# Talking-heads attention and a leaky MLP: cast and remainder of a regrouped tile two groups ahead of its mixing, and a weight piece narrowed every third step

## The chip, the cores and the metric

One core of one Trainium2 chip runs the whole program. The time is device microseconds from the first to the last instruction of one execution, as the median of several runs. The engines are TensorE (PE for its matmuls, PEld for its weight loads), VectorE (DVE), ScalarE (ACT), GpSimd (POOL) and SyncE (SP), which issues nearly all DMAs from one queue.

## The reference

```python
def _attn_ref(q, k, v, w_pre, w_post):              # q, k, v: 4 x 12 x 448 x 64
    scores = scale * np.matmul(q, k.transpose(0, 1, 3, 2))
    scores = np.einsum('bhij,hg->bgij', scores, w_pre)
    scores = scores - np.max(scores, axis=-1, keepdims=True)
    attn = np.exp(scores)
    attn = attn / (np.sum(attn, axis=-1, keepdims=True) + 1e-09)
    attn = np.einsum('bhij,hg->bgij', attn, w_post)
    return np.matmul(attn, v)

def _moe_ref(x, w_in, w_out):                       # x: 1792 x 768, w_in: 768 x 2048
    h = x @ w_in
    return np.maximum(0.01 * h, h) @ w_out
```

The output of the attention, with the heads side by side, is the `x` of the MLP. The MLP's weights arrive as 64-bit floats, two 32-bit words each, and the kernel has to make 32-bit floats of them: it calls that narrowing.

## The kernel before

**Attention.** The 448 queries of each of the 4 batches are cut into chunks of 120, 120, 120 and 88 rows, 16 chunks in all. A chunk is walked in 12 slots (`t` in the main loop). In slots 0 to 5 `scores(n + 1, h)` makes the scores of two heads of the next chunk: two matmuls into `pss` (the query as a rounded part `qhi` and a remainder `qlo`), copied by ScalarE into `st`. At the end of slot 5 all twelve heads are there, and `regroup` (line 205) starts transfers from `st` to tiles `rt` in which 10 queries by 12 heads lie on 120 partitions: four at slot 5, two each at slots 7, 8, 9 and 10. `softmax(n, s, g)` takes one such group: ScalarE rounds `rt` to `rhi` (line 218), the remainder `rlo` is made by GpSimd, or by VectorE where g is 3 (line 219), three matmuls mix the heads into `psm` in the order hi, lo, hi (line 222), VectorE takes the maximum (223), ScalarE the exponential (224), and after the last group of four the normalising factors go into `kp` (235 to 237). In slot t the loop calls `softmax` for a group that is four slots ahead: in slots 6 and 7 the last two of chunk n, in slots 8 to 11 the first four of chunk n + 1. `mix` (264, copied out at 272) mixes the heads again three slots behind the slot, and `values` (290) multiplies by v in slots 6 to 11. I call slots 6 to 9, where the work goes over from one chunk's groups to the next one's, the turn.

In slot 6 `prep_q(n + 2)` splits the queries of the chunk after next: two casts on ScalarE (`qhi`, line 177) and two subtractions on GpSimd (`qlo`, line 178), half of the heads each. In two of four chunks of a batch `prep_k` splits the keys of the next batch (lines 153 and 154, VectorE and GpSimd).

**Narrowing.** `w_moe` is cut into 64 pieces of 128 x 384 weights: 16 blocks f, of which pieces 0 and 1 are the half for the first matmul and 2 and 3 that for the second. `Narrow` loads one (line 91, 384 KB, tile `craw`), `scale` has two activations on ScalarE (101, 102, into `z` and `w`), `place` three VectorE operations (108, 111, 114, into `top` and `exp`), `join` two GpSimd operations and the store of 192 KB to `w_dram` (117, 118, 119). The first instruction of each stage is pinned by `keep_in_program_order`. Within the attention a piece is started every fifth slot, its stages come four, five and six slots later, and `craw` and `w` have two buffers each: 36 pieces (four each of blocks 0 and 1, two each of the others). The other 28, two each of blocks 2 to 15, are narrowed in the first pass of the MLP, by `load_w` (line 333 and those before it).

**MLP.** 4 batches x 16 blocks: `hidden(i)` is 18 matmuls into `psh`, `project(i)` 18 into `pso` (line 347), each weight split into `wh` and `wl` by VectorE (340, 341). `load_w` reads 384 KB halves `wr` back from `w_dram`, except where the piece is narrowed on the spot.

**What sets the order.** TensorE's instructions run in the order in which the program gives them. On the other engines the framework orders them at build time with its own estimate of the times: of the instructions that it takes to be ready, the one that stands first in the program goes first. On the chip each engine and SyncE's queue then run strictly in that order. The tiles' pools bring the waits: a tile can be written only when the last reader of its buffer is done.

Of the kernel before, what the change touches and what calls it, by code (L numbers as in the profile page):

```python
# [8 lines left out]
F32 = mybir.dt.float32  # L9
F32R = mybir.dt.float32r  # L10
U32 = mybir.dt.uint32
# [12 lines left out]
PIECE = 384  # L24
LATE = 3
EARLY = 2
# [7 lines left out]
def kernel(  # L34
# [10 lines left out]
    nc = tc.nc  # L45
    B, P, NJ, H, D = v.shape
    S = k.shape[3]
# [4 lines left out]
    RH = ROWS * H  # L52
    SLOTS = 3 * NJ
# [25 lines left out]
    class Narrow:  # L79
# [7 lines left out]
        def __init__(self, pool, f, j, w=None):  # L87
            at = slice(PIECE * j, PIECE * (j + 1))
            self.pool, self.w, self.dst = pool, w, w_dram[f][:, at]
            self.raw = pool.tile([P, PIECE, 2], U32, tag="raw", name="craw", bufs=2)  # L90
            nc.sync.dma_start(self.raw.rearrange("p n w -> p (n w)"), w_moe[f, :, at].bitcast(U32))
# [5 lines left out]
        def scale(self, pin):  # L97
            if self.w is None:
                self.w = self.pool.tile([P, PIECE], F32, tag="w", name="w", bufs=2)
# [26 lines left out]
    p_rs = pool("rs", 3)  # L126
# [79 lines left out]

    def softmax(n, s, g):
# [7 lines left out]
        raw = r_t.pop((n, s, g))  # L215
        hi = p_rs.tile([RH, S], F32R, tag="hi", name="rhi")
        lo = p_rs.tile([RH, S], F32R, tag="lo", name="rlo")
        nc.scalar.copy(hi[:kk], raw[:kk])  # L218
        (nc.vector if g == 3 else nc.gpsimd).tensor_sub(lo[:kk], raw[:kk], hi[:kk].bitcast(F32))  # L219
# [205 lines left out]
    for n in range(NCK):  # L425
# [4 lines left out]
        for t in range(SLOTS):  # L430
# [7 lines left out]
            if (n * SLOTS + t) % 5 == 0 and pieces and not last:  # L438
                with tc.issue_after(last_dma[0].ins):
                    narrowing.append(Narrow(p_c, *pieces.pop(0)))  # L440
            if n % NB == NB - 2 and b + 1 < B:
                load_k(b + 1, t)
# [26 lines left out]
            flush = n * SLOTS + t == (NCK - 1) * SLOTS - 1  # L469
            phase = (n * SLOTS + t) % 5  # L470
            if phase == 4 and narrowing:
                narrowing[0].scale(tc.keep_in_program_order)
            if phase == 0 and narrowing and narrowing[0].w is not None or flush and narrowing:
                narrowing[0].place(tc.keep_in_program_order)
            if phase == 1 and narrowing and narrowing[0].w is not None or flush and narrowing:
                narrowing.pop(0).join(tc.keep_in_program_order)
# [95 lines left out]
```

## Time and profile before

| | us |
|---|---|
| median of 3 runs (1104.58 to 1112.42) | 1104.62 |
| the profiled execution, its own time | 1114.43 |
| span of the profiled execution | 1112.7 |
| TensorE busy in the span | 997.6 |
| VectorE busy | 739.7 |
| ScalarE busy | 511.4 |
| GpSimd busy | 431.9 |

The profiled execution took 1114.43 us, 1.7 us more than its span from the first to the last instruction, and 0.9% more than the median. The attention fills the span to about 605 us, the MLP the rest. A matmul's end is modelled in the profile, so a busy TensorE is not TensorE at its peak.

### The profile page before, as it was taken

How to read it: one execution, taken by the hardware profiler on the slowest of the kernel's cores; microseconds unless marked ns; L12 is line 12 of the kernel's file. 1: busy time of each engine (PE TensorE's matmuls, PEld its weight loads, DVE VectorE, ACT ScalarE, POOL GpSimd, SP SyncE). 2: the span in 40 equal slices, each digit the busy share in tenths (PEclk: the TensorE clock that was granted, in tenths of full speed). 3: DMA queues.
4: the chain of work that ended last, by engine and by line, in shares of the span. 5: the costliest groups of instructions: out<-in, count | busy, mean ns of one | idle time of the engine just before them, and what ended most of it. 6: DMA issues, size and time to landing. Idle time of an engine off the chain costs nothing.

```text
span 1112.7 us, 17708 instructions
## 1 busy us (share of the span) xinstructions
PE 997.6 (90%) x6564; PEld 836.3 (75%) x6564; DVE 739.7 (66%) x1210; ACT 511.4 (46%) x1131; POOL 431.9 (39%) x356
## 2 busy tenths in 40 slices
PE   4879689898788997898998988889999999999998
PEld 2667577676566875777777877778999999999997
DVE  5567967569566776666676698797555655565553
ACT  3777577666457775777673333331111211121111
POOL 4576855558556477545542256650000000000000
PEclk9989899988889998999998999999999999999999
DMA  4645534743543564326544566556333633353331
GB/s 159 249 155 190 169 116 157 226 174 101 163 170 113 155 207 161 128 100 207 174 160 140 152 179 192 176 169 208 104 109 104 200 100 113 103 160 100 114 88 62
DMA packets 93770, 167.10 MB, mean 150 GB/s; under 512 B 26740, under 2 KB 68724, under 8 KB 93172
## 3 DMA queue, kind: packets, MB, share of 16 engines
q1 hardware_dynamic: 91956, 163.23, 45.8%
q10 hardware_dynamic: 1728, 2.75, 0.7%
q8 instruction: 51, 0.84, 0.3%
q14 instruction: 35, 0.29, 0.1%
HBM read 103.82 MB, written 23.59 MB: 115 GB/s over the span
## 4 chain that ended last, share of the span: by engine, by line
PE 52%; DVE 15%; DMA 9%; ACT 6%; POOL 5%; issue 5%; SPq 1%; ACTq 0%; POOLq 0%; DVEq 0%
PE psh L347 17%; PE pso L347 16%; PE psa L264 6%; PE psx L290 5%; PE psm L222 5%; DMA craw<-in_w_moe 4%; PE pss L194 3%; DMA w_dram<-w 2%; POOL rlo L219 2%; DMA rt<-st 2%; DVE kst L153 2%; DVE stat L223 2%; DVE wh L340 2%; ACT et L224 2%; POOL qlo L178 1%
## 5 line engine op out<-in xcount | busy, mean ns | idle before, releaser
L219 POOL TENSOR_TENSOR rlo<-rt,rhi 120x448 fp32r<-120x448 f32 x144 | 172.3, 1207 | 117.9 <-ACT rhi L218 109.5
L264 PE MATMUL psa<-kp,et 120*128 120x120 f32 (+2 forms) x1800 | 193.4, 269 | 2.8 <-DVE at L272 2.4
L264 PEld LDWEIGHTS psa<-kp,et 120*128 120x128 f32 (+2 forms) x1800 | 174.5, 179 | 28.5 <-issue 14.0
L340 DVE CAST wh<-wr 128x768 fp32r<-128x768 f32 x128 | 81.9, 640 | 142.0 <-PE psh L347 94.4
L222 PE MATMUL psm<-rhi,kpre 120*120 120x448 f32 x360 | 150.7, 419 | 28.2 <-ACT et L224 14.2
L223 DVE TENSOR_REDUCE stat<-psm 120x1 f32<-120x448 f32 x180 | 111.2, 618 | 70.9 <-PE psm L222 69.8
L347 PE MATMUL pso<-gh,wl 128*128 128x448 f32 x384 | 141.3, 370 | 13.7 <-DVE wl L341 13.7
L358 ACT ACTIVATE t<-psh 128x448 f32<-128x448 f32 x64 | 34.8, 544 | 247.8 <-PE psh L347 247.8
L347 PE MATMUL psh<-xh,wl 128*128 128x448 f32 x384 | 141.7, 369 | 1.9 <-DVE wl L341 1.5
L347 PE MATMUL psh<-xl,wh 128*128 128x448 f32 x384 | 141.2, 368 | 0.0
L347 PE MATMUL pso<-gh,wh 128*128 128x448 f32 x384 | 141.1, 367 | 0.0
L347 PE MATMUL psh<-xh,wh 128*128 128x448 f32 x384 | 141.1, 367 | 0.0
L347 PE MATMUL pso<-gl,wh 128*128 128x448 f32 x384 | 141.1, 367 | 0.0
L224 ACT ACTIVATE et<-psm,stat 120x448 f32<-120x448 f32 x180 | 115.6, 642 | 49.3 <-DVE stat L223 45.2
L218 ACT CAST rhi<-rt 120x448 fp32r<-120x448 f32 x180 | 101.6, 571 | 54.0 <-PE psm L222 27.4
L341 DVE TENSOR_TENSOR wl<-wr,wh 128x768 fp32r<-128x768 f32 x128 | 124.9, 976 | 1.6
L195 ACT ACTIVATE st<-pss 120x448 f32<-120x448 f32 (+1 forms) x192 | 105.8, 557 | 9.0 <-PE pss L194 8.9
L222 PE MATMUL psm<-rlo,kpre 120*120 120x448 f32 x180 | 73.3, 407 | 37.9 <-POOL rlo L219 37.9
L194 PE MATMUL pss<-kst,qlo 128*120 128x448 f32 (+1 forms) x192 | 83.6, 436 | 26.0 <-ACT st L195 14.5
L222 PEld LDWEIGHTS psm<-rhi,kpre 120*120 120x120 f32 x360 | 71.4, 198 | 42.9 <-ACT et L224 18.2
L347 PEld LDWEIGHTS pso<-gh,wl 128*128 128x128 f32 x384 | 72.1, 188 | 25.0 <-issue 18.2
L272 DVE COPY at<-psa 128x480 f32<-128x480 f32 (+2 forms) x112 | 68.2, 609 | 32.3 <-PE psa L264 31.9
(64 smaller groups left out, 1650.5 us busy)
## 6 DMA issues: line engine op xcount, KB each, us to landing
wr<-w_dram SPq DMA_DIRECT2D x114, 384.0 KB
rt<-st SPq DMA_DIRECT2D x176, 210.0 KB
craw<-in_w_moe SPq DMA_DIRECT2D x64, 384.0 KB
kraw<-in_k SPq DMA_DIRECT2D x48, 224.0 KB
qraw<-in_q SPq DMA_DIRECT2D x11, 720.0 KB
w_dram<-w SPq DMA_DIRECT2D x36, 192.0 KB
vt<-in_v SPq DMA_DIRECT2D x4, 1536.0 KB
xr<-x_dram SPq DMA_DIRECT2D x24, 224.0 KB
```

Source lines behind the costliest of these rows:

```text
L194: nc.tensor.matmul(ps[:m, :S], w[:, h, :m], k_t[b, h], start=i == 0, stop=i == 1)
L195: nc.scalar.activation(s_t[n][:m, h, :], ps[:m, :S], AF.Copy, scale=scale)
L218: nc.scalar.copy(hi[:kk], raw[:kk])
L219: (nc.vector if g == 3 else nc.gpsimd).tensor_sub(lo[:kk], raw[:kk], hi[:kk].bitcast(F32))
L222: nc.tensor.matmul(ps[:kk, :S], kpre[w][:kk, :sg[g][1], :], x[:kk], start=i == 0, stop=i == 2)
L223: nc.vector.tensor_reduce(st[:kk, 0, g:g + 1], ps[:kk, :S], axis=AX.X, op=ALU.max, negate=True)
L224: nc.scalar.activation(e[:kk], ps[:kk, :S], AF.Exp, bias=st[:kk, 0, g:g + 1], accum_out=st[:kk, 1, g:g + 1])
L264: nc.tensor.matmul(ps[p0:p0 + np, w * g:w * g + nh * r], es[g][:r * H, c * P:c * P + np], kp[:r * H, g, h::step, :r], start=True, stop=True,)
L272: copy(at[:, :, i:i + full * ROWS].rearrange("p h (g r) -> p g h r", r=ROWS), ps[:, :w * full].rearrange("p (g h r) -> p g h r", h=nh, r=R ...
L340: nc.vector.tensor_copy(hi, raw)
L341: nc.vector.tensor_sub(lo, raw, hi.bitcast(F32))
L347: nc.tensor.matmul(ps, w[a][:, c * P:(c + 1) * P], x[e], start=first and j == 0, stop=last and j == 2)
```

## The change

Two things. The two steps that make `rhi` and `rlo` leave `softmax` for a function `split`, and `softmax` of a group first calls `split` for every group up to two places on in the sequence of all groups, as far as its regrouping was started; the tiles have four buffers in place of three. And a piece of the weights is started every third slot in place of every fifth, with three buffers each for `craw` and `w`; blocks 0 to 13 give four pieces and 14 and 15 two, so 60 of the 64 are narrowed in the attention and four (of blocks 14 and 15) in the MLP. Each piece goes through its stages four, five and six slots after its start, as before, and whatever is left at slot 11 of the last chunk but one is finished there.

```diff
+AHEAD = 2
-EARLY = 2
+EARLY = 14
...
-            self.raw = pool.tile([P, PIECE, 2], U32, tag="raw", name="craw", bufs=2)
+            self.raw = pool.tile([P, PIECE, 2], U32, tag="raw", name="craw", bufs=3)
...
-                self.w = self.pool.tile([P, PIECE], F32, tag="w", name="w", bufs=2)
+                self.w = self.pool.tile([P, PIECE], F32, tag="w", name="w", bufs=3)
...
-    p_rs = pool("rs", 3)
+    p_rs = pool("rs", 4)
...
+    sequence = [(n, s, g) for n in range(NCK) for s in range(3) for g in range(len(chunks[n][3][s]))]
+    split_t = {"next": 0}
+
+    def split(n, s, g):
+        kk = chunks[n][3][s][g][1] * H
+        raw = r_t.pop((n, s, g))
+        hi = p_rs.tile([RH, S], F32R, tag="hi", name="rhi")
+        lo = p_rs.tile([RH, S], F32R, tag="lo", name="rlo")
+        nc.scalar.copy(hi[:kk], raw[:kk])
+        (nc.vector if g == 3 else nc.gpsimd).tensor_sub(lo[:kk], raw[:kk], hi[:kk].bitcast(F32))
+        split_t[n, s, g] = hi, lo
...
-        raw = r_t.pop((n, s, g))
-        hi = p_rs.tile([RH, S], F32R, tag="hi", name="rhi")
-        lo = p_rs.tile([RH, S], F32R, tag="lo", name="rlo")
-        nc.scalar.copy(hi[:kk], raw[:kk])
-        (nc.vector if g == 3 else nc.gpsimd).tensor_sub(lo[:kk], raw[:kk], hi[:kk].bitcast(F32))
+        while split_t["next"] <= min(sequence.index((n, s, g)) + AHEAD, len(sequence) - 1):
+            if sequence[split_t["next"]] not in r_t:
+                break
+            split(*sequence[split_t["next"]])
+            split_t["next"] += 1
+        hi, lo = split_t.pop((n, s, g))
...
-            if (n * SLOTS + t) % 5 == 0 and pieces and not last:
+            if (n * SLOTS + t) % 3 == 0 and pieces and not last:
...
+                    narrowing[-1].at = n * SLOTS + t
...
-            phase = (n * SLOTS + t) % 5
-            if phase == 4 and narrowing:
-                narrowing[0].scale(tc.keep_in_program_order)
-            if phase == 0 and narrowing and narrowing[0].w is not None or flush and narrowing:
-                narrowing[0].place(tc.keep_in_program_order)
-            if phase == 1 and narrowing and narrowing[0].w is not None or flush and narrowing:
-                narrowing.pop(0).join(tc.keep_in_program_order)
+            at = n * SLOTS + t
+            for piece in list(narrowing):
+                while piece.stage < 3 and (piece.stage or at - piece.at >= 4 or at == (NCK - 1) * SLOTS - 1):
+                    (piece.scale, piece.place, piece.join)[piece.stage](tc.keep_in_program_order)
+                    piece.stage += 1
+                    if at < (NCK - 1) * SLOTS - 1:
+                        break
+                if piece.stage == 3:
+                    narrowing.remove(piece)
```

## Rows read from the trace of the kernel before

**Rows 1.** The page: busy time, share of the span and instructions of each engine, and the 40 slices of the span (27.8 us each) for TensorE, and the clock that it was granted (9 is 90% or more of full speed).

```profile
PE 997.6 (90%) x6564; PEld 836.3 (75%) x6564; DVE 739.7 (66%) x1210; ACT 511.4 (46%) x1131; POOL 431.9 (39%) x356
...
PE   4879689898788997898998988889999999999998
...
PEclk9989899988889998999998999999999999999999
```

**Rows 2.** Windows over three stretches, first the attention, then the first steps of the MLP, then the rest of it: start and end, length, then for each engine its busy time and instructions, then the granted clock, the busy share of the DMA engines and GB/s.

```profile
60.00:605.00 545.00, 473.93 (x3991) 374.63 (x3993) 380.20 (x661) 364.21 (x842) 326.40 (x271) 0.92 0.48 158
605.00:750.00 145.00, 129.98 (x718) 114.11 (x714) 117.46 (x188) 47.07 (x99) 73.41 (x56) 1.00 0.55 169
750.00:1108.00 358.00, 357.43 (x1728) 324.18 (x1728) 206.81 (x308) 63.80 (x117) 0.00 (x0) 1.00 0.39 119
```

**Rows 3.** Waits of TensorE's matmuls from 60 to 605 us: who waited for whom, us in total, times, the longest.

```profile
PE psm L222 <- POOL rlo L219: 36.9, 16, 4.6
PE psm L222 <- ACT et L224: 13.8, 9, 2.9
...
PE psm L222 <- ACT rhi L218: 7.2, 5, 2.1
```

**Rows 4.** Windows over four chunks of the attention, each from the first regrouping transfer of one chunk to that of the next (columns as in rows 2).

```profile
87.60:125.28 37.68, 33.01 (x302) 25.50 (x299) 30.14 (x50) 24.87 (x59) 28.11 (x24) 1.00 0.52 173
125.28:161.86 36.58, 29.33 (x234) 23.25 (x234) 25.31 (x42) 23.54 (x54) 23.86 (x20) 0.91 0.49 163
387.03:423.01 35.98, 31.95 (x288) 24.77 (x288) 28.90 (x48) 25.43 (x60) 27.05 (x23) 1.00 0.57 186
495.95:530.88 34.93, 31.34 (x278) 25.44 (x278) 24.66 (x43) 26.78 (x61) 19.50 (x16) 0.95 0.57 189
```

**Rows 5.** Timeline of one turn from chunk to chunk, 494 to 508 us: start and length in us, engine, line, operation, tiles, shapes, count, and in brackets the idle time before it and what ended it.

```profile
495.95 3.28 SPq L205 DMA_DIRECT2D rt<-st  x4
496.27 2.90 ACT L177 CAST qhi<-qraw 128x720 fp32r<-128x720 f32 x2
...
497.84 4.57 POOL L178 TENSOR_TENSOR qlo<-qraw,qhi 128x720 fp32r<-128x720 f32 x2 [5.67 <-ACT qhi L177]
...
499.07 0.64 ACT L224 ACTIVATE et<-psm,stat 120x448 f32<-120x448 f32 x1
...
499.69 0.57 ACT L218 CAST rhi<-rt 120x448 fp32r<-120x448 f32 x1
...
500.31 0.47 PE L222 MATMUL psm<-rhi,kpre 120*120 120x448 f32 x1
...
500.77 1.04 ACT L218 CAST rhi<-rt 120x448 fp32r<-120x448 f32 x2
502.38 1.24 POOL L219 TENSOR_TENSOR rlo<-rt,rhi 120x448 fp32r<-120x448 f32 x1
...
503.67 0.46 PE L222 MATMUL psm<-rlo,kpre 120*120 120x448 f32 x1 [2.89 <-POOL rlo L219]
...
504.55 3.02 POOL L219 TENSOR_TENSOR rlo<-rt,rhi 120x448 fp32r<-120x448 f32 x2
...
507.19 0.71 PE L222 MATMUL psm<-rhi,kpre 120*120 120x448 f32 x1
```

**Rows 6.** Groups of instructions from 60 to 605 us, of every engine: line, engine, operation, tiles, shapes, count, then busy us and mean ns of one, then the idle time of the engine before them and what ended most of it.

```profile
L219 POOL TENSOR_TENSOR rlo<-rt,rhi 120x448 fp32r<-120x448 f32 x135 | 162.1, 1211 | 112.4 <-ACT rhi L218 104.1 <-DMA w_dram<-w 3.3 <-DMA x_dram<-xo 3.0
...
L218 ACT CAST rhi<-rt 120x448 fp32r<-120x448 f32 x165 | 93.1, 571 | 48.0 <-PE psm L222 25.3 <-POOL rlo L219 13.0 <-DMA rt<-st 4.9
...
L178 POOL TENSOR_TENSOR qlo<-qraw,qhi 128x720 fp32r<-128x720 f32 (+1 forms) x26 | 51.3, 1995 | 32.4 <-ACT qhi L177 32.1
...
L118 POOL TENSOR_TENSOR w<-w,top 128x384 f32<-128x384 f32 x36 | 38.5, 1070 | 1.2
L117 POOL TENSOR_TENSOR w<-w,exp 128x384 f32<-128x384 f32 x36 | 37.1, 1031 | 44.0 <-DVE exp L114 36.8 <-PE psm L222 6.1 <-DVE stat L236 0.9
...
L111 DVE SCALAR_TENSOR_TENSOR top<-z,top 128x384 uint32<-128x384 uint32 x35 | 32.1, 917 | 0.4
...
L114 DVE TENSOR_SCALAR exp<-top 128x384 uint32<-128x384 uint32 x35 | 21.3, 609 | 0.4
L101 ACT ACTIVATE z<-craw 128x384 f32<-128x384 f32 x35 | 19.5, 558 | 0.0
L102 ACT ACTIVATE w<-craw 128x384 f32<-128x384 uint32 x34 | 19.0, 560 | 59.1 <-DMA w_dram<-w 32.6 <-DMA craw<-in_w_moe 20.2 <-POOL rlo L219 6.3
...
L108 DVE TENSOR_SCALAR top<-z 128x384 uint32<-128x384 uint32 x35 | 18.0, 514 | 3.8 <-ACT z L101 3.7
```

**Rows 7.** The line of the second step of `place`, over the whole span: shortest, median and longest of one in ns, first and last start, shapes.

```profile
L111 DVE SCALAR_TENSOR_TENSOR top<-z,top x64: 543/550/2316, 54.1 to 744.3; 128x384 uint32<-128x384 uint32 x64
```

**Rows 8.** Waits of SyncE's queue from 60 to 605 us, the longest in total: us, times, the longest.

```profile
SPq L119 <- POOL w L118: 130.1, 25, 12.3
```

**Rows 9.** The chain of waits over the whole span, some pieces of it in the MLP: start, us, what it is.

```profile
666.43 3.14 DMA craw<-in_w_moe
...
675.10 3.13 DMA craw<-in_w_moe
...
773.35 3.72 PE pso L347 x18
...
780.79 3.72 PE pso L347 x18
```

More of the change, by code (lines that the diff above doesn't have):

```diff
@@ L88, in __init__ @@
             at = slice(PIECE * j, PIECE * (j + 1))
+            self.at, self.stage = None, 0
             self.pool, self.w, self.dst = pool, w, w_dram[f][:, at]
-            self.raw = pool.tile([P, PIECE, 2], U32, tag="raw", name="craw", bufs=2)
+            self.raw = pool.tile([P, PIECE, 2], U32, tag="raw", name="craw", bufs=3)
             nc.sync.dma_start(self.raw.rearrange("p n w -> p (n w)"), w_moe[f, :, at].bitcast(U32))
@@ L467 @@
                 store_x(n - 1, 0)
-            flush = n * SLOTS + t == (NCK - 1) * SLOTS - 1
-            phase = (n * SLOTS + t) % 5
-            if phase == 4 and narrowing:
-                narrowing[0].scale(tc.keep_in_program_order)
-            if phase == 0 and narrowing and narrowing[0].w is not None or flush and narrowing:
-                narrowing[0].place(tc.keep_in_program_order)
-            if phase == 1 and narrowing and narrowing[0].w is not None or flush and narrowing:
-                narrowing.pop(0).join(tc.keep_in_program_order)
+            at = n * SLOTS + t
[7 more added lines that the diff above has]
+                    narrowing.remove(piece)
             if n % NB == NB - 2 and b + 1 < B and t > 1:
```

## The prediction

> **What bounds the kernel now.** I read the page first, then windows by stage, then TensorE's waits, then one turn in the timeline. The page shows TensorE busy for 90% of the span, with a ragged first half and a full second one, and the granted clock low in spots of the first half only [rows 1]. The windows say the same by stage [rows 2]: from 750 us on TensorE is busy for 357.43 of 358 us and nothing can be won; from 605 to 750 it is busy for 129.98 of 145 while VectorE is busy for 117.46; in the attention for 473.93 of 545, at a mean clock of 0.92. In the attention no engine is full (VectorE 380, ScalarE 364, GpSimd 326 of 545), so it is bound by the order in which TensorE's inputs arrive.
>
> The largest of its waits is for `rlo`, 36.9 us in 16 waits; 7.2 us more go to `rhi` and 13.8 us to the exponential [rows 3]. The 16 are nearly one per turn. The turn at 495.95 us shows how one arises [rows 5]: the regrouping is issued at 495.95, ScalarE does the two query casts (2.90 us), GpSimd the two query remainders from 497.84 for 4.57 us; `rhi` of the first new group is ready at 500.26, but its `rlo` starts at 502.38, when GpSimd is through, and TensorE has waited 2.89 us at 503.67. Behind the wait the clock falls: a matmul that took 0.46 us is one of 0.71 us at 507.19. Of four chunks two hold a clock of 1.00 all the way, the others 0.91 and 0.95 [rows 4]. A clock of 0.92 over 545 us, with levels of 1.2 and 2.4 GHz, is 2 x 0.08 x 545 = 87 us at the lower level.
>
> In the first steps of the MLP the chain runs over a loaded piece, 8.67 us from one step to the next (666.43 to 675.10), against 7.44 us later (773.35 to 780.79) [rows 9].
>
> **The change part by part.** The sums are on the profiled execution, 1114.43 us, which is 0.9% above the median of 1104.62; at the end I multiply by 1104.62 / 1114.43 = 0.9912.
>
> *MLP.* Of the 14 steps that narrow two pieces each, 12 (blocks 2 to 13) now read one `wr` of 384 KB instead, as the later steps do. 12 x (8.67 - 7.44) = -14.8 us. The two that stay (blocks 14, 15) stay at 8.67. Bounds: if the start of the stage is held up by something else anyway, two steps less, -12.3; if the two last are absorbed by slack, -17.2. I take -14.8.
>
> *The wait at the turn.* In the steady part of a chunk nothing is won: `rhi` already runs ahead as far as three buffers let it, and TensorE's waits are at the turn. There the transfer cannot come earlier: the source is complete only at the end of slot 5. What changes is rank. `split` of the first new group now stands in slot 6 ahead of `prep_q`, where its cast and remainder stood in slot 8 behind it. The query work is still ready sooner, since it needs no transfer, so the first cast and the first half of `qlo` go first; the second half (mean 1.995 us [rows 6]) should now come behind `rlo`. In the turn of [rows 5] the first half ends near 500.1 and `rhi` at 500.26, so `rlo` could start at 500.3 in place of 502.38, about one half. Bounds for the 15 turns: nothing, if the build-time order still takes `qlo` twice because it expects the transfer later; all 44.1 us of waits for `rlo` and `rhi`. One half each where the wait is that long, somewhat less in the short ones: 20 us, near the middle. What is late next: the second group's `rlo` now has the second half of `qlo` ahead of it, 2.0 + 1.2 us [rows 6], against the 3.5 us from one group's matmuls to the next at the lower clock (503.67 to 507.19 [rows 5]) and, as my estimate, 2.8 at the higher; some 0.4 us a turn, +6 us. Together -14 us.
>
> *The clock.* 87 us at half speed cost at most 43.5 us; TensorE is idle for 13% of the attention [rows 2], so about 37. That two chunks stay at 1.00 shows that it can go wholly; with waits as they are it stays. I take 40%, -15 us.
>
> *24 more pieces in the attention.* Each brings ScalarE 0.558 + 0.560 = 1.12 us, VectorE 0.514 + 0.917 + 0.609 = 2.04 us, GpSimd 1.031 + 1.070 = 2.10 us [rows 6], so 27, 49 and 50 us in 545: ScalarE goes to 391, VectorE to 429, GpSimd to 377, none full. Not all of this is hidden, as all three queues are served in order and each carries a step of the loop from `psm` to the exponential. ScalarE also waits at line 102, which is queued ahead of casts and exponentials: 59.1 us for 36 pieces, over half of it for the store of the piece whose `w` it takes [rows 6], 1.64 us a piece. Behind it wait `et`, `st` and the copies, and TensorE for those. The new buffers don't relieve this: three at a distance of three slots give 9 slots, two at five gave 10. Bounds of one piece on the path: nothing (below nothing I exclude, as it only adds work), and all that it takes of ScalarE, 1.12 + 1.64 = 2.76 us. The own instructions count where the engine is busy anyway, 364 of 545, so 1.12 x 0.67 = 0.75; of the waits I count nothing more, since a lead of two groups lets TensorE go on meanwhile. 24 x 0.75 = +18 us; the ends are 0 and 66.
>
> *What I cost at nothing.* The DMA engines go from 158 GB/s by 24 x 576 KB in 545 us, 26 GB/s, at a share of 0.48 [rows 2]; without that room the regrouping would land later, at every turn. SyncE gets 48 more issues; it stands 130.1 us before stores whose `join` isn't done [rows 8], with regroupings and loads queued behind, and the cover is that the regrouped groups past the first four are used slots later. The fourth buffer of `rhi` and `rlo` adds no instruction. The pinned `join` in GpSimd's queue waits for `place` (36.8 us [rows 6]) and holds up the remainders behind it; there will be more such waits, and the remainders two groups ahead are their cover.
>
> One place of the Trainium skill speaks against the change, and no term of the sum hangs on it. The rows show that the second operation of `place` takes 550 ns in the median and 2316 at most [rows 7], and 917 on average in the attention. The Trainium skill, SBUF — State Buffer, "Who interferes with whom", has it that VectorE operations with two inputs in SBUF, or in a two-port mode, exclude a GpSimd operation that reads SBUF, and that the loser is blocked entirely. By that rule the 50 us of added GpSimd work could lengthen VectorE's by up to 50 us beside the 49 that I count, 479 of 545 us; this row agrees that it happens, but VectorE would still not be full.
>
> **Sum:** -14.8 - 14 - 15 + 18 = -25.8 us: 1114.43 - 25.8 = 1088.6, times 0.9912 is 1079.
>
> **The rivals.**
> A, the forecast: 1079, its own range 1062 to 1095.
> B, the lead does nothing at the turn, since `rlo` is held by the landing and by `qlo` still ranked first in time. For it: the query remainder is ready 2 us before the first cast of the new group. Against: rank decides when GpSimd becomes free between the two halves. -14.8 + 18 = +3.2: 1108.
> C, slower: ScalarE's queue becomes the bound. Line 102 waits for a store or a load at the head of the queue, and each piece costs its whole 2.76 us: +66 - 14.8 - 29 = +22: 1127. It decides from (14.8 + 29) / 24 = 1.8 us a piece on. For it: 59.1 us of such waits already. Against: most are in slots where TensorE does not wait for ScalarE, 7.2 + 13.8 us of waits for `rhi` and `et` in all [rows 3].
> D, the turn is freed altogether: waits of 44 and the whole 37 us of clock go: -81 + 18 - 14.8 = -78: 1027. For it: the two causes hang together, a turn without a wait keeps its clock. Against: `qlo` and the transfer stay where they are. What lies between A and D is likelier than its end.
>
> **How the numbers follow.** A 0.55, B 0.17, C 0.11, D and the way to it 0.17. A measurement of this kernel tells about 1%, 11 us. Faster by more: A but for 0.03, and D: 0.69. Within: that 0.03 and B but for 0.03: 0.17. Slower: C and the rest of B: 0.14. The range of 8 in 10 leaves out the far half of D (0.08) and C (0.11): 1050 to 1112.
>
> **What would show it.** MLP: steps of 7.44 us from the first on, narrowing in two of them only; by this term alone some 15 us. Turn: `rlo` of the first new group between the two halves of `qlo`, waits for `rlo` near 17 us in place of 36.9, fewer low spots of the clock, a mean of 0.94 to 0.95 in the attention. Pieces: VectorE near 430 and GpSimd near 377 us in the attention, idle time before line 102 in proportion to 60 pieces, near 98 us, but TensorE's waits for `et` and `st` not above 40 us. I am wrong if `qlo` still precedes `rlo` in both halves (B), if waits for `et`, `st` and `rhi` grow past what `rlo` loses (C), or if the attention's clock goes to 0.98 (D).

## The result and the profile after

The changed kernel takes 1122.13 us (median of 4, 1116.48 to 1125.64) against 1106.95 us for the kernel before, a ratio of 1.0113 [1.0064, 1.0161]: 1.1% slower, where 1079 us, 2.3% faster, was forecast, and 10 us past the end of the range.

The page of the changed kernel: engines, and the 40 slices (27.9 us each) for TensorE and its granted clock.

```profile
PE 992.8 (89%) x6564; PEld 842.0 (76%) x6564; DVE 740.3 (66%) x1210; ACT 511.8 (46%) x1131; POOL 423.0 (38%) x356
...
PE   3879687898787889688989999999999999999998
...
PEclk8889998899887899889999899999999999999999
```

Beside [rows 1], the ragged part of TensorE's row has become longer, and the clock low in more slices; what follows is solid. The border between the two parts is the first matmul of the MLP: 605.8 us before, 636.0 after. So the attention is 30.2 us longer, and the MLP, from there to the end of the span, 28.0 us shorter (506.9 to 478.9).

Windows of the changed kernel: the attention as in [rows 2], then the first 151 us of the MLP and the rest (start and end, length, busy time and instructions of PE, PEld, DVE, ACT and POOL, granted clock, share of the DMA engines, GB/s).

```profile
60.00:605.00 545.00, 457.48 (x3741) 360.08 (x3743) 394.68 (x681) 372.71 (x856) 367.01 (x308) 0.91 0.53 173
636.00:787.20 151.20, 151.20 (x827) 138.82 (x827) 97.59 (x151) 31.55 (x61) 10.02 (x8) 1.00 0.48 142
787.20:1108.00 320.80, 320.80 (x1584) 297.35 (x1584) 183.49 (x272) 56.24 (x102) 0.00 (x0) 1.00 0.38 113
```

The same view over the whole attention, first of the kernel before and then of the changed one.

```profile
60.00:605.80 545.80, 474.73 (x4001) 375.15 (x4001) 380.72 (x661) 364.51 (x842) 326.40 (x271) 0.92 0.48 158
```

```profile
60.00:636.00 576.00, 484.16 (x4014) 381.57 (x4014) 420.55 (x730) 385.73 (x888) 379.23 (x318) 0.91 0.54 173
```

The MLP starts without a gap: 151.20 us busy of 151.20, where [rows 2] had 129.98 of 145. In the attention TensorE is idle for 576.00 - 484.16 = 91.8 us, against 71.1 (545.8 - 474.7) before; that is 20.7 of the 30.2 us. The other 9.5 us are matmuls that took longer, at a mean clock of 0.91 in place of 0.92.

Waits of TensorE's matmuls in the changed kernel, 60 to 605 us (us in total, times, the longest).

```profile
PE psm L237 <- POOL rlo L218: 45.9, 15, 5.0
PE pss L196 <- ACT st L197: 18.7, 20, 2.2
PE psm L237 <- ACT et L239: 12.8, 7, 6.2
PE psm L237 <- ACT rhi L217: 11.0, 8, 2.0
```

Against [rows 3] the waits for `rlo` rose from 36.9 to 45.9 us and those for `rhi` from 7.2 to 11.0; both were to fall. `et` is hardly changed. `st` rose from 10.7 to 18.7; its row in the kernel before:

```profile
PE pss L194 <- ACT st L195: 10.7, 14, 1.7
```

Where in a chunk the added waits lie can be counted in the two traces: from a chunk's first regrouping issue to 15 us behind it they rose from 45.7 to 56.8 us in total, and in the rest of the chunk, where they are mostly for `st` and `et`, from 25.7 to 36.6. So the turn has only half of the loss.

The turn of the same chunk as in [rows 5], in the changed kernel (start and length, engine, line, operation, tiles, count, idle time before).

```profile
483.18 3.29 SPq L207 DMA_DIRECT2D rt<-st  x4
...
484.60 4.30 POOL L180 TENSOR_TENSOR qlo<-qraw,qhi 128x720 fp32r<-128x720 f32 x2 [3.26 <-ACT qhi L179]
...
486.88 1.51 ACT L217 CAST rhi<-rt 120x448 fp32r<-120x448 f32 x3
...
487.51 0.47 PE L237 MATMUL psm<-rhi,kpre 120*120 120x448 f32 x1 [0.88 <-ACT rhi L217]
...
488.88 1.03 POOL L119 TENSOR_TENSOR w<-w,exp 128x384 f32<-128x384 f32 x1
...
489.87 3.70 POOL L218 TENSOR_TENSOR rlo<-rt,rhi 120x448 fp32r<-120x448 f32 x3
...
491.43 0.73 PE L237 MATMUL psm<-rlo,kpre 120*120 120x448 f32 x1 [3.45 <-POOL rlo L218]
...
493.53 0.99 POOL L120 TENSOR_TENSOR w<-w,top 128x384 f32<-128x384 f32 x1
```

Both halves of `qlo` (line 180) still come ahead of the first `rlo`. And where [rows 5] has `rlo` right behind them, there is now an operation of `join` (line 119) in between: `rlo` starts 6.7 us after the transfer's issue (483.18) in place of 6.4, and its matmul 8.25 us after it in place of 7.7, having waited 3.45 us in place of 2.89. The other operation of `join` (line 120) comes behind three `rlo`. In all 14 turns with query work both halves of `qlo` come first, and an operation of `join` stands between them and the first `rlo` or between the two halves; in the kernel before that is so in 5 of the 14.

Groups of lines of the changed kernel, 60 to 605 us (busy us, mean ns of one, idle time of the engine before them and what ended it).

```profile
L120 POOL TENSOR_TENSOR w<-w,top 128x384 f32<-128x384 f32 x57 | 61.9, 1086 | 1.8
...
L119 POOL TENSOR_TENSOR w<-w,exp 128x384 f32<-128x384 f32 x56 | 58.9, 1051 | 57.5 <-DVE exp L116 56.2 <-DVE stat L251 1.3
...
L110 DVE TENSOR_SCALAR top<-z 128x384 uint32<-128x384 uint32 x57 | 43.0, 755 | 13.5 <-POOL w L120 12.3 <-ACT z L103 0.9
...
L113 DVE SCALAR_TENSOR_TENSOR top<-z,top 128x384 uint32<-128x384 uint32 x56 | 41.8, 747 | 0.9
...
L104 ACT ACTIVATE w<-craw 128x384 f32<-128x384 uint32 x57 | 31.7, 558 | 55.9 <-DMA w_dram<-w 28.3 <-issue 16.5 <-DMA craw<-in_w_moe 6.4
...
L116 DVE TENSOR_SCALAR exp<-top 128x384 uint32<-128x384 uint32 x56 | 30.3, 542 | 0.9
```

An instruction costs what it did in [rows 6]: `join` 1051 and 1086 ns, `place` 755 + 747 + 542 = 2044 ns in place of 2040. So the price per instruction was right, and also the busy time that follows from it: over the whole attention 421 us of VectorE and 379 of GpSimd, forecast near 430 and 377. What the forecast missed is what those operations hold up.

### The profile page after: what moved, and what is told of

Read it like the earlier page. It is cut to its first block, busy times and chain, and to the rows that moved or that the text cites. A ratio compares the mean times of both kernels' runs of the same rounds, so it can differ in the third digit from the quotient of the medians.

```text
span 1114.8 us, 17666 instructions
## 1 busy us (share of the span) xinstructions
PE 992.8 (89%) x6564; PEld 842.0 (76%) x6564; DVE 740.3 (66%) x1210; ACT 511.8 (46%) x1131; POOL 423.0 (38%) x356
## 4 chain that ended last, share of the span: by engine, by line
PE 54%; DVE 13%; DMA 10%; POOL 7%; issue 6%; ACT 6%; SPq 3%; POOLq 0%; ACTq 0%; DVEq 0%
PE psh L362 21%; PE pso L362 21%; PE psa L279 4%; PE psx L305 3%; POOL rlo L218 3%; DMA w_dram<-w 3%; DMA rt<-st 3%; PE psm L237 3%; SPq L207 3%; DVE kst L155 2%; DMA kraw<-in_k 2%; DVE stat L238 2%; ACT et L239 2%; POOL w L119 2%; DVE top L110 2%
## 5 line engine op out<-in xcount | busy, mean ns | idle before, releaser
L355 DVE CAST wh<-wr 128x768 fp32r<-128x768 f32 x128 | 72.8, 569 | 167.5 <-PE psh L362 112.7
L217 ACT CAST rhi<-rt 120x448 fp32r<-120x448 f32 x180 | 99.9, 567 | 43.4 <-PE psm L237 24.9
L196 PE MATMUL pss<-kst,qlo 128*120 128x448 f32 (+1 forms) x192 | 85.6, 446 | 34.0 <-ACT st L197 22.4
L237 PEld LDWEIGHTS psm<-rhi,kpre 120*120 120x120 f32 x360 | 71.5, 199 | 49.2 <-ACT rhi L217 20.2
L119 POOL TENSOR_TENSOR w<-w,exp 128x384 f32<-128x384 f32 x60 | 62.8, 1047 | 64.6 <-DVE exp L116 63.3
```

What stands on the lines that cost most here:

```text
L119: pin(nc.gpsimd.tensor_mul(self.w, self.w, self.exp.bitcast(F32)))
L196: nc.tensor.matmul(ps[:m, :S], w[:, h, :m], k_t[b, h], start=i == 0, stop=i == 1)
L237: nc.tensor.matmul(ps[:kk, :S], kpre[w][:kk, :sg[g][1], :], x[:kk], start=i == 0, stop=i == 2)
L355: nc.vector.tensor_copy(hi, raw)
```

## The experiments

The theory after the result: **the turn's order.** TensorE waits at the turn for what GpSimd does last, the clock follows these waits, and the lead does not change GpSimd's order, since the query work is ready before the new group's. The added pieces lose time by operations in in-order queues, above all `join` ahead of `rlo` (of this last part the experiments bear out only half, as will be seen). The rivals: that the lead itself does harm; that ScalarE's queue at line 104 is the cost (rival C); that SyncE's queue is, with stores that wait for `join`; that it is VectorE. All ratios are to the kernel before on the same chip. "End of attention" is the first matmul of the MLP in the profiled execution, of which there is one for each kernel. Executions of one kernel differ by up to 14 us (e1: 1098.26 to 1112.29), so a few us between two rows of the last four columns prove nothing by themselves.

| kernel | ratio [95%] | end of attention, us | TensorE idle from 60 us to there | clock there | waits for `rlo`, 60 to 605 |
|---|---|---|---|---|---|
| before | 1 | 605.8 | 71.1 | 0.92 | 36.9 |
| after | 1.0113 [1.0064, 1.0161] | 636.0 | 91.8 | 0.91 | 45.9 |
| e1_split_only | 0.9979 [0.9943, 1.0015] | 598.8 | 67.0 | 0.92 | 38.1 |
| e2_pieces_only | 1.0232 [1.0197, 1.0267] | 649.2 | 97.9 | 0.91 | 47.3 |
| e3_after_qlate | 0.9828 [0.9791, 0.9865] | 599.0 | 69.9 | 0.95 | 15.2 |
| e4_before_qlate | 0.9754 [0.9711, 0.9798] | 575.7 | 53.5 | 0.96 | 14.5 |
| e5_no_gpsimd | 0.9840 [0.9783, 0.9898] | 604.6 | 70.5 | 0.92 | 30.8 |
| e6_no_vector | 0.9985 [0.9959, 1.0011] | 619.5 | 83.6 | 0.92 | 42.4 |
| e7_four_buffers | 1.0058 [1.0029, 1.0086] | 634.3 | 84.1 | 0.90 | 43.0 |
| e8_lead_qlate | 0.9700 [0.9656, 0.9745] | 568.8 | 49.0 | 0.96 | 7.6 |
| e9_free_store | 1.0186 [1.0121, 1.0251] | 634.3 | 93.0 | 0.92 | 44.8 |
| e10_off_turn | 0.9942 [0.9911, 0.9974] | 621.4 | 78.4 | 0.91 | 37.3 |
| e11_every_fourth | 0.9739 [0.9664, 0.9815] | 571.6 | 58.8 | 0.96 | 5.9 |
| e12_join_on_vector | 0.9683 [0.9624, 0.9741] | 591.9 | 68.4 | 0.96 | 10.6 |

### The two parts, each alone

**e1_split_only**: the lead and the fourth buffers, with the old narrowing.

```diff
-EARLY = 14
+EARLY = 2
...
-            if (n * SLOTS + t) % 3 == 0 and pieces and not last:
+            if (n * SLOTS + t) % 5 == 0 and pieces and not last:
```

(with two buffers of `craw` and `w`, and the stages of before)

> The lead of two groups alone: the function that splits two groups ahead and the fourth buffer, with the narrowing of the kernel before (36 pieces, every fifth slot, two buffers). Theory B (rank does nothing at the turn, because GpSimd takes both halves of the query remainder before the first rlo of the new chunk in either program): the time of the kernel before within 0.5%, waits of TensorE for rlo near 37 us, first rlo of a chunk still some 6 us after its transfer's issue. Forecast's theory: 25 to 30 us faster than before. A third way: the lead itself costs, because casts two groups ahead stand in ScalarE's queue before the exponentials: some 10 us slower than before.

0.9979 [0.9943, 1.0015]: no difference that can be measured. Its turn in the timeline, the same chunk again:

```profile
489.40 3.28 SPq L207 DMA_DIRECT2D rt<-st  x4
...
491.28 4.67 POOL L180 TENSOR_TENSOR qlo<-qraw,qhi 128x720 fp32r<-128x720 f32 x2 [6.44 <-ACT qhi L179]
...
493.15 1.01 ACT L217 CAST rhi<-rt 120x448 fp32r<-120x448 f32 x2
...
495.91 2.36 POOL L218 TENSOR_TENSOR rlo<-rt,rhi 120x448 fp32r<-120x448 f32 x2
```

The transfer is issued at 489.40 and `rhi` is there at about 493.7, but both halves of `qlo` run first, until 495.95, and `rlo` starts 6.5 us after the issue, as in [rows 5] (6.4). The lead changed nothing at the turn: waits for `rlo` are 38.1 us, 36.9 before. (The attention of this one execution is 7.0 us shorter, which the ratio does not bear out.)

**e2_pieces_only**: the 60 pieces without the lead.

```diff
-AHEAD = 2
+AHEAD = 0
...
-    p_rs = pool("rs", 4)
+    p_rs = pool("rs", 3)
```

> The pieces alone: 60 of 64 narrowed in the attention with three buffers, the split of a group made in its own softmax call, with three buffers as before. If the pieces are what costs: the attention about 30 us longer than before, the MLP about 17 us shorter, so about 12 us slower than before in all, like the changed kernel. If the lead is the cost: about 17 us less the pieces' own 18, so the time of before. Within: if the lead covers some of the pieces' waits, this is slower than the changed kernel by up to 20 us.

1.0232 [1.0197, 1.0267]. The attention ends 43.4 us later than before, 1.8 us for each of 24 pieces; with the lead it was 30.2, or 1.26 us. So the lead does no harm, and by the ratios (2.3% and 1.1% slower) it shields the pieces a little; the loss is all from the pieces.

### Moving the queries out of the turn

**e3_after_qlate** and **e4_before_qlate**: the changed kernel and the kernel before with `prep_q(n + 2)` called in slot 8 or 9, its casts pinned there, so that GpSimd's `qlo` cannot come ahead of the turn's `rlo`.

```diff
-            if t == HALF and n + 2 < NCK:
-                prep_q(n + 2)
+            if t == 8 and n + 2 < NCK:                            # 9 in e4
+                prep_q(n + 2, pin=tc.keep_in_program_order)
...
-            hi_op(to_hi, dealt)
+            pin(hi_op(to_hi, dealt))
```

> The changed kernel with the split of the queries moved from slot 6 to slot 8 and its casts pinned behind what stands ahead of them, so that the first remainders of the new chunk come before the query remainders on GpSimd. If the turn is set by GpSimd's order: first rlo about 4 us after its transfer's issue in place of 6.3, TensorE's waits for rlo from 46 to about 15 us, clock in the attention from 0.90 to about 0.95, 30 to 45 us faster than the changed kernel. If the transfer or ScalarE sets the turn: within 8 us of the changed kernel.

> The kernel before with the split of the queries moved from slot 6 to slot 9 and its casts pinned in the same way, nothing else. If the turn is set by GpSimd's order: TensorE's waits for rlo from 37 to about 12 us and 25 to 40 us faster than before. If not, or if the queries now come late for the next scores: the time of before or slower by up to 10 us, with new waits of the score matmuls for qlo.

0.9828 [0.9791, 0.9865] and 0.9754 [0.9711, 0.9798]. The turn of e4, the same chunk:

```profile
471.35 3.28 SPq L205 DMA_DIRECT2D rt<-st  x4
...
474.17 0.57 ACT L218 CAST rhi<-rt 120x448 fp32r<-120x448 f32 x1 [1.40 <-DMA rt<-st]
...
474.82 1.14 POOL L219 TENSOR_TENSOR rlo<-rt,rhi 120x448 fp32r<-120x448 f32 x1 [7.51 <-ACT rhi L218]
...
476.01 0.46 PE L222 MATMUL psm<-rlo,kpre 120*120 120x448 f32 x1
...
481.72 2.93 ACT L177 CAST qhi<-qraw 128x720 fp32r<-128x720 f32 x2
...
483.28 4.21 POOL L178 TENSOR_TENSOR qlo<-qraw,qhi 128x720 fp32r<-128x720 f32 x2 [0.85 <-ACT qhi L177]
```

`rlo` starts 3.5 us after the issue, right behind `rhi`, and its matmul (476.01) 4.7 us after it, where [rows 5] has 7.7; the queries follow at 481.72. TensorE's two largest waits in e4, 60 to 605 us:

```profile
PE pss L194 <- ACT st L195: 20.1, 25, 1.7
PE psm L222 <- POOL rlo L219: 14.5, 16, 1.8
```

Waits for `rlo` fall by 22 us in e4 and by 31 in e3, and the clock over the attention rises from 0.92 to 0.96 and from 0.91 to 0.95. In e4 the attention is 30.1 us shorter: 17.6 us less idle time (71.1 to 53.5) and 12.5 us shorter matmuls. That the two go together is what the forecast said of the turn; only the change does not bring it about. What is late next in e4 is `st`, 20.1 us.

**e8_lead_qlate**: the lead and the late queries, with the old narrowing, so e1 and e3 together.

> The lead of two groups with the queries split in slot 8 and pinned, and the narrowing of the kernel before (36 pieces). The late split of the queries alone gave 2.5% on the kernel before. If the lead adds to it (it gave 7 us of attention without it): 1068 to 1074. If both only free the same turn: 1078, as the late split alone. If casts two groups ahead now wait in ScalarE's queue for transfers that have not landed (39.7 us of such waits where lead and late split stood together): 1080 to 1088.

0.9700 [0.9656, 0.9745], 3% below before. The window over its attention:

```profile
60.00:568.80 508.80, 459.84 (x3997) 366.42 (x3996) 372.09 (x661) 365.15 (x843) 334.79 (x271) 0.96 0.52 170
```

The attention is 6.9 us shorter than in e4 (575.7 to 568.8), and waits for `rlo` are 7.6 in place of 14.5. But from before to e1, with the turn as it was, the attention became shorter by as much; e4 splits the queries in slot 9 and e8 in slot 8; and the intervals of the two ratios overlap. So a gain of the lead at the freed turn is not shown. From e8 to e3 there are only the 24 pieces: the attention grows by 30.2 us, 1.26 us a piece, turn or no turn. In e3 the first `rlo` of most chunks starts 3.4 to 4.3 us after the issue, soon behind `rhi`, and the pieces cost the same; so `join` ahead of the first `rlo` cannot be all that they cost.

### Which resource the pieces use up

**e5_no_gpsimd** and **e6_no_vector**: without `join`'s two operations on GpSimd, and without `place`'s three on VectorE.

```diff
-            pin(nc.gpsimd.tensor_mul(self.w, self.w, self.exp.bitcast(F32)))
-            nc.gpsimd.tensor_add(self.w, self.w, self.top.bitcast(F32))
             nc.sync.dma_start(self.dst, self.w)                   # e5
```

In e6 the body of `place` is empty, and `join` takes `z` in place of `exp` and `top`.

> The changed kernel without the two GpSimd operations of join: the piece is stored as ScalarE left it (the upper word's share and the product are left out). Pieces cost 43 us of attention alone and 30 with the lead. Theory G (GpSimd's queue, and what its operations hold up on VectorE, charges the pieces): 25 to 40 us faster than the changed kernel, and VectorE's place shorter, toward 1.45 us a piece. Theory S (ScalarE's queue, waiting at the second activation for a store or a load, charges them): at most 10 us faster, by the join that stood between the query remainders and the first rlo of a turn. Theory V (VectorE's own work): at most 10 us.

> The changed kernel without the three VectorE operations of place; join multiplies and adds z itself, so GpSimd's work stays. Theory V: 25 to 40 us faster than the changed kernel. Theory G: part of it, 5 to 15 us, since GpSimd no longer stands before a place that isn't done (57.9 us of such waits in the changed kernel). Theory S: within 5 us.

0.9840 [0.9783, 0.9898] and 0.9985 [0.9959, 1.0011]. Against the changed kernel the attention is 31.4 us shorter without GpSimd's 2.1 us a piece, and 16.5 us without VectorE's 2.0. Together these are more than the 30.2 us in question: they overlap, both kernels also lack the operations of the 36 pieces that before has in its attention, and e6 also takes away the 56.2 us for which `join` waited for `exp`. GpSimd's share is about twice the other. One part of e5's expectation failed: `place` was to fall toward 1.45 us a piece. Its operations in e5:

```profile
L113 DVE SCALAR_TENSOR_TENSOR top<-z,top 128x384 uint32<-128x384 uint32 x59 | 47.3, 801 | 0.8
...
L116 DVE TENSOR_SCALAR exp<-top 128x384 uint32<-128x384 uint32 x59 | 38.0, 645 | 1.0
...
L110 DVE TENSOR_SCALAR top<-z 128x384 uint32<-128x384 uint32 x59 | 29.6, 502 | 3.0 <-ACT z L103 3.0
```

801 + 645 + 502 = 1948 ns, against 2044 with `join`: the removal of all of `join` gives back 0.1 us of each 2.0. The reason is in the trace of the changed kernel: from 60 to 605 us no operation of `place` runs beside one of `join`, but many run beside GpSimd's `rlo`, `qlo` and `kst`, and those take longer. Of line 113, 34 with nothing on GpSimd beside them took 552 ns on average (561 at most), and 22 with something beside them 1049 ns; of line 110 it is 350 and 1029 ns, of line 116 354 and 1229. The maximum of line 238, whose input `psm` lies in PSUM, takes 616 ns either way. Two of line 113 in the changed kernel, the second with an `rlo` of GpSimd beside it:

```profile
53.12 0.55 DVE L113 SCALAR_TENSOR_TENSOR top<-z,top 128x384 uint32<-128x384 uint32 x1
...
80.34 1.20 POOL L218 TENSOR_TENSOR rlo<-rt,rhi 120x448 fp32r<-120x448 f32 x1 [0.50 <-ACT rhi L217]
80.57 1.39 DVE L113 SCALAR_TENSOR_TENSOR top<-z,top 128x384 uint32<-128x384 uint32 x1
```

The Trainium skill (SBUF — State Buffer, "Who interferes with whom") has it that a VectorE operation with two inputs in SBUF and a GpSimd operation that reads SBUF exclude each other; 552 against 1049 ns at line 113 agrees with it. So of the 2.04 us of `place` some 0.8 are this lengthening (552 + 350 + 354 = 1256 ns without it), before the change as after it, and none of that is due to `join`.

**e7_four_buffers**: four buffers each of `craw` and `w` in the changed kernel, for what ScalarE waits for at line 104.

```diff
-name="craw", bufs=3)
+name="craw", bufs=4)
...
-name="w", bufs=3)
+name="w", bufs=4)
```

> The changed kernel with four buffers in place of three for the loaded piece and for the one that is made, so 12 slots before a buffer is taken again. Theory S: ScalarE's idle time before its second activation falls from about 55 us to under 20, and the time by 15 to 25 us. Theories G and V: those waits fall as well, but the time stays within 6 us.

1.0058 [1.0029, 1.0086], some 0.5% below the changed kernel, with intervals that overlap, but the waits that were to fall below 20 us did not (ScalarE's waits, 60 to 605 us):

```profile
ACT w L104 <- DMA craw<-in_w_moe: 43.8, 29, 3.2
ACT w L104 <- DMA w_dram<-w: 34.5, 16, 5.6
```

They are 78.3 us, against 28.3 + 6.4 in the changed kernel and 32.6 + 20.2 in before. More waiting at line 104, and yet not slower than the changed kernel: ScalarE's idle time there is not what TensorE pays for. That expectation failed, and with it rival C's mechanism, which rests on the waits at this line. Why the waits grew with more buffers is not known. In e5 such waits were still larger, 84.1 us for the load alone, in a kernel faster than before.

**e9_free_store**: GpSimd's operations as they are, but with a tile of their own as output, and the store takes the piece as ScalarE left it, so that it no longer waits for them.

```diff
+            done = self.pool.tile([P, PIECE], F32, tag="done", name="done")
-            pin(nc.gpsimd.tensor_mul(self.w, self.w, self.exp.bitcast(F32)))
-            nc.gpsimd.tensor_add(self.w, self.w, self.top.bitcast(F32))
+            pin(nc.gpsimd.tensor_mul(done, self.w, self.exp.bitcast(F32)))
+            nc.gpsimd.tensor_add(done, done, self.top.bitcast(F32))
```

> The changed kernel with GpSimd's two operations of join kept in number, size and place, but writing to a tile of their own, and the store taking the piece as ScalarE left it, so that SyncE's queue no longer waits for join (155.9 us of such waits in the changed kernel). It tells what the 33 us were that went when join's operations went. Theory G (GpSimd's time and order): within 8 us of the changed kernel, 1115 to 1125. Theory Q (SyncE's queue, where regroupings and loads stand behind a store that waits): close to the kernel without join, 1088 to 1098.

1.0186 [1.0121, 1.0251]: no gain. The median, 1127.4, lies even above the 1115 to 1125 expected for GpSimd's time and order; the attention is 1.7 us shorter than the changed kernel's, and the MLP, at the slower of two rates (last section), 9.9 longer. SyncE's largest wait in the changed kernel was the store's for `join`; the regroupings' for `st` stands below it:

```profile
SPq L121 <- POOL w L120: 155.9, 38, 8.8
...
SPq L207 <- ACT st L197: 26.8, 13, 3.2
```

In e9 it is gone; the queue waits for ScalarE instead, for `st` of the regrouping and for `w`:

```profile
SPq L208 <- ACT st L198: 100.4, 14, 9.7
SPq L122 <- ACT w L104: 92.7, 27, 6.4
```

At 14 regroupings the queue now stands ready before the scores are, for 100.4 us in all (26.8 us at 13 of them in the changed kernel), and TensorE gains nothing by it. So the 155.9 us of SyncE's waiting were not on the path: what e5 gained came from GpSimd's operations, not from the store.

### Where the pieces stand

**e10_off_turn**: pieces started one slot later, in slots 1, 4, 7 and 10.

```diff
-            if (n * SLOTS + t) % 3 == 0 and pieces and not last:
+            if (n * SLOTS + t) % 3 == 1 and pieces and not last:
```

> The changed kernel with pieces started in slots 1, 4, 7 and 10 in place of 0, 3, 6 and 9, so that join falls into slots 7, 10, 1 and 4 and not into slot 6, where it stands between the query remainders and the first rlo. If the place at the turn is what the pieces cost: first rlo from 6.5 to 5.6 us after its transfer's issue, 10 to 15 us faster than the changed kernel. If it is GpSimd's time wherever it lies: within 5 us.

0.9942 [0.9911, 0.9974]; the median is 22.4 us below the changed kernel's, for the same work (0.9942 / 1.0113 is 1.7% less, 19 us). Three divides twelve: `join` comes in slots 6, 9, 0 and 3 of every chunk, of which 6 is in the turn, and with the shift in 7, 10, 1 and 4. Before, with five, it fell in slot 6 in one chunk of five. A turn of e10 on GpSimd, behind a transfer issued at 467.54:

```profile
469.41 4.31 POOL L180 TENSOR_TENSOR qlo<-qraw,qhi 128x720 fp32r<-128x720 f32 x2 [3.01 <-ACT qhi L179]
473.69 2.65 POOL L218 TENSOR_TENSOR rlo<-rt,rhi 120x448 fp32r<-120x448 f32 x2
476.30 1.38 POOL L119 TENSOR_TENSOR w<-w,exp 128x384 f32<-128x384 f32 x1
```

Here `rlo` follows `qlo` directly, as in 11 of the 14 turns. Waits for `rlo` fell to 37.3 us. But in most turns `rlo` still starts 4.5 to 6.5 us after the issue, against 5.3 to 6.6 in the changed kernel, and in three turns, those with GpSimd's work for the next batch's keys, 10.7 to 11.9, which is later than the 8.8 there. So the slot in which a piece's stages run matters, and the first `rlo` explains only part of why. The edit moves the load, `scale`, `place`, `join` and the store together; that it is the place of `join` which counts is not shown.

**e11_every_fourth**: e3 with a piece every fourth slot, 44 in the attention.

```diff
-EARLY = 14
+EARLY = 6
...
-            if (n * SLOTS + t) % 3 == 0 and pieces and not last:
+            if (n * SLOTS + t) % 4 == 0 and pieces and not last:
```

> Lead of two groups and the late split of the queries, with a piece every fourth slot: 44 in the attention (blocks 0 to 5 whole), 20 in the MLP. With 36 it took 1072, with 60 1089. If each piece costs the same: 8/24 of the way, about 1077 to 1079. If the price rises only when GpSimd gets full: 1070 to 1074. If it lies in the coincidence with the turn, which a distance of three or four slots has in every chunk and five has not: 1084 or more.

0.9739 [0.9664, 0.9815], between e8 (36 pieces, 0.970) and e3 (60, 0.9828), with the attention 2.8 us longer than in e8. 44 pieces are no better than 36 either: in the profiled executions the MLP did not become shorter (501.1 us, 500.3 in e8), and why is open. With a distance of four slots `join` comes in slot 6 of every chunk, and 1084 us or more were expected if that coincidence were the price; the median is 1076.93. With the queries out of the way it isn't.

**e12_join_on_vector**: e3 with `join` on VectorE.

```diff
-            pin(nc.gpsimd.tensor_mul(self.w, self.w, self.exp.bitcast(F32)))
-            nc.gpsimd.tensor_add(self.w, self.w, self.top.bitcast(F32))
+            pin(nc.vector.tensor_mul(self.w, self.w, self.exp.bitcast(F32)))
+            nc.vector.tensor_add(self.w, self.w, self.top.bitcast(F32))
```

> Lead of two groups, the late split of the queries, 60 pieces, and join's two operations on VectorE in place of GpSimd (with join on GpSimd 1089). If GpSimd's time and order charge the pieces: faster than that by 5 to 15 us, although VectorE takes about 1.3 us more a piece. If VectorE is now the next to be full (427 of 545 us before, some 500 with it): slower, 1095 to 1115.

0.9683 [0.9624, 0.9741], level with e8. Its attention:

```profile
60.00:591.90 531.90, 463.47 (x4037) 367.15 (x4037) 484.50 (x849) 385.92 (x894) 264.89 (x200) 0.96 0.57 188
```

VectorE is at 484.50 of 531.90 us, GpSimd at 264.89 in place of e3's 387.18, and the attention 7.1 us shorter than e3's. The medians are 16.4 us apart, but in the traces 10.7 of the difference lies in the MLP, whose code the two share and which e3 ran at the slower rate; so at most the 7.1 us can be put down to `join`. 24 pieces now cost 23.1 us (591.9 - 568.8), which is what they save later. With 60 pieces one is no better off than with 36, even so.

## Why the prediction was wrong

**The MLP: right in kind, larger than its bounds.** -14.8 us were forecast from the steps of [rows 9]. TensorE's idle time in the first stretch went from 15.0 us (145 - 129.98) to nothing; that the two last steps cost nothing either was within the bounds. The whole stage lost 28.0 us, because in the profiled execution of after the matmuls were also quicker. Pieces of the chain of the changed kernel, answering to the last of [rows 9]:

```profile
774.62 3.65 PE pso L362 x18
...
781.92 3.65 PE pso L362 x18
```

From one step to the next 7.30 us (774.62 to 781.92) in place of 7.44, both at a granted clock of 1.00. That is no gain of the change: e1, e4 and e8, with the old narrowing, came to the quicker rate too (median matmul 365 ns in place of 368), and there the stage took 500.1, 500.3 and 500.3 us. So of the 28.0 us some 6.7 are the rate (506.9 to 500.2, or 48 steps of 0.14 us behind the narrowing), and 21.4 the pieces (500.3 to 478.9), about 0.9 us for each of 24. That is more than the upper end, 17.2: 15.4 us of it are idle time, as forecast (20.0 us in e8's MLP, 4.6 in that of after), and the other 6 us are matmuls that ran slower beside the narrowing, which the forecast didn't count. The two profiled executions are just 2.1 us apart (1114.43 and 1116.48) and the medians 15.2, as the one of before is slower than all four of its timed executions and the one of after the fastest of its four; whether the rate has a part in that no other trace shows.

**The wait at the turn: the step that failed first.** "The second half (mean 1.995 us [rows 6]) should now come behind `rlo`." It did not: -14 us was forecast, and +12.8 came (`rlo` and `rhi`: 44.1 to 56.9 us). The build-time order takes what is ready first, and place in the program decides only between instructions that are ready. The query remainder needs ScalarE's casts alone, and the new group a transfer; e1 shows the order unchanged. (What the framework took for the times is not on record, so this reason is argued.) The chip's own times left no room either: in all 14 turns of the changed kernel the first half of `qlo` ended before the first `rhi` was there, in the turn above 3.53 and 4.28 us after the issue. The prediction's figures said the same of [rows 5], 500.1 and 500.26: when GpSimd came free, the second half was ready and `rlo` was not. This is rival B, which had 0.17; its argument, that the remainder is ready first, was in the text. The rest of the step was sound: e3 and e4 take exactly this wait away, and gain 2.5% on before (e4) and, as the quotient of the ratios, 2.8% on after (e3).

**The clock** follows from it: 0.94 to 0.95 forecast, 0.91 measured, so -15 became a part of the +9.5 us of slower matmuls. With the turn freed it did rise, to 0.95 and 0.96. It goes with the waits at the turn and not with idle time as such: e1 was idle for 67.0 us at 0.92 and e12 for 68.4 us at 0.96, with 38.1 and 10.6 us of waits for `rlo`.

**The pieces: the step that failed second.** 0.75 us a piece was taken, between 0 and 2.76; 1.8 us were measured without the lead and 1.26 with it, against about 0.9 saved in the MLP. Wrong was not only the size but the engine: the price was made from ScalarE's instructions, and GpSimd's were put at nothing, since "the remainders two groups ahead are their cover". Without `join` on GpSimd the attention is 31.4 us shorter and the ratio 2.7% lower (e5). At the turn there is no such cover, as no remainder is ahead there, and `join` came to stand ahead of the first `rlo` in every turn. But that is part of the price only: half of the added waits lie later in the chunk, and with the turn freed the pieces cost the same 30.2 us (e8 to e3). That the slot counts is shown by e10 (1.7%); that it is neither line 104 nor the store, by e7 and e9. 1122 is near rival C's 1127, but C's mechanism is not what happened: idle time before line 104 is 55.9 us, not the 98 that the forecast gave for 60 pieces, and the waits for `et` and `st` are 31.5 us, under the 40 that it named as a limit.

**Sum.** Forecast -25.8 us on the profiled execution: -14.8 in the MLP and -11 in the attention. Found: +2.1, -28.0 in the MLP, of which about 7 are the rate, and +30.2 in the attention.

What stays open: why e10 gains more than its earlier first `rlo` gives, what TensorE's longer waits for `st` and `et` outside the turn go back to, why e11's MLP gains nothing by eight pieces less, and how the 1.26 us a piece divide into GpSimd's, VectorE's (e6) and ScalarE's parts when the turn is free. The parts that were taken out singly overlap.

## What to carry to other kernels

An earlier place in the program does not move an instruction ahead of one that is ready sooner: where a build-time order takes what is ready, the work that stands in the way has to be pinned behind the critical one. The price of side work in an in-order queue cannot be read from the engine's mean load: here 24 pieces on engines busy for 66 to 73% of the attention cost 30 us of it, and the same pieces one slot later 19 us less in the whole. An engine's long waits prove nothing until someone is seen to wait for that engine: freeing SyncE's queue of 155.9 us of waits for `join` gained nothing. And a busy time is not the work alone: `place` takes 1.26 us when GpSimd is still and 2.04 on average in this mix.

## What the runs showed of the hardware

At a granted clock of 1.00 and with TensorE busy without a gap, some executions ran 36 matmuls of 448 columns in 7.44 us, others in 7.30 (206.7 and 202.8 ns each). The rate does not go with the MLP's code: before, e3 and e9 had the first in the solid part of the MLP, after and the other ten the second, with e3 and after, or before and e4, alike in the MLP. Nor is it fixed for an execution: e9's MLP began at the second rate and went on at the first. Over a whole MLP it is 9 us, nearly 1% of the time, which the clock's column does not show; so a difference of that size between two profiled executions need not be one of their kernels. Each kernel has one trace, so what rate its other executions had is not known.

The three operations of `place` (128x384, all in SBUF) took 350, 552 and 354 ns when nothing ran on GpSimd beside them, never above 364 or 561, and 1.0 to 1.2 us on average when something did. The same split, and the same times without company to within 5 ns, is in the traces of all the other kernels that have `place`.
